# A token mixer behind a windowed attention: tap products added in pairs on VectorE, transposed sums stored as they are, and the softmax, the split of u and the stores planned as separate items

## The chip, the cores and the metric

The kernel runs on one core of a Trainium2 chip. The metric is the device time of one execution in microseconds (us), from the first to the last instruction of the program and the little around them. Engines are named as in the profile: PE is TensorE (PEld its weight loads), DVE is VectorE, ACT is ScalarE, POOL is GpSimd, SP is SyncE, which here only issues transfers.

## What is computed

```python
# attention over a window of 7 past rows; B, S, D = 8, 4096, 192; 8 heads of 24 channels
w = softmax(weight_gen, axis=-1)                        # [8, 4096, 8, 7]
out[b, s, h, :] = sum_k w[b, s, h, k] * x_pad[b, s + k, h, :]
# then, with x = out, a token mixer and a channel mixer
h  = relu(x.transpose(0, 2, 1) @ w_tok1) @ w_tok2       # 4096 -> 256 -> 4096
u  = x + h.transpose(0, 2, 1)
out = u + relu(u @ w_ch1) @ w_ch2                       # 192 -> 1536 -> 192
```

The weights of the mixers are 64-bit floats. From the 32-bit numbers made of them the products on PE are built in three parts, high by high, high by low and low by high (token1 of the first two batches is plain).

## The kernel before

The 8 x 4096 rows are cut into 64 chunks of 512 rows (`g` or `m`, 0 to 63), eight to a batch. A chunk is held as [128 partitions, 4 rows, 192 channels]. For each chunk there are these steps:

- **Softmax** (L163 to L180), for two chunks at a time: five VectorE instructions and one exponential on ScalarE.
- **Attention** (`attention`, L196): seven tap products, x shifted by k rows times the weight of tap k (`product`, L203), each 128x768 on VectorE. The first goes into the sum `xa`; each of the other six goes into one of four buffers `pr` (PR, L46), and GpSimd issues a transfer that adds the buffer to `xa` in memory (`add_dma`, L220). The next addition into the same `xa` waits until the one before has landed, and a product that needs a buffer waits until an addition has emptied it.
- **Turning**: VectorE transposes the finished `xa` in blocks of 32x32 (`turn`, L283), ScalarE moves the blocks with 24 copies of 32x128 (`move`, L289, L293) into `ts`, and ScalarE's queue stores `ts` to memory (`keep`, L272). Later SP loads it as `xb` with two transfers (`load_xt`, L309). For the first eight chunks PE does the turning (`turn_first`).
- **token1** (L480 to L502): PE multiplies the first token weights with `xa`; VectorE adds the result up over the eight chunks of a batch in `h1s`. From batch 2 on `xa` is first split into a high and a low part, `xh` (L257 on ScalarE, L260 on VectorE).
- **token2** (`token2`, L506): ten matmuls (L513) into PSUM, three VectorE additions with `xb` (L520 to L522) that make u, and its split into high and low parts (two VectorE and four ScalarE instructions, L524 to L529), all issued at once behind one another.
- **Channel mixer**, three quarters per chunk: `channel1` (24 matmuls, L544 and L549, into two PSUM tiles `ph`; each is then evicted as `h` by ScalarE, L552, and VectorE, L553), and `channel2` (20 matmuls, L567, into the one PSUM tile `acc`) for the quarter before.
- **Store** (`store`, L572): three VectorE additions empty `acc` (L577 to L579), two transposes (L581, L582), 12 ScalarE copies (L589), two transfers on ScalarE's queue (L599).

During the prologue and the first eight chunks ScalarE and VectorE also convert the weights from 64 bits (`convert`, L137; `convert_w2`, L395 on, with L404 and L405 for its high and low part).

PSUM has three tiles of kind `w`, used in turn by `ph`, token1 and token2, and one `acc`. So PE's next `channel1` waits for the VectorE instruction at L553 of an earlier quarter, and the first `channel2` of a chunk waits for L579 of the chunk before.

Each engine works its instructions off in the order in which they were written. That order is made while the program is built, by a planner in the same file: it keeps an estimated clock per engine (`at`), issues the PE work quarter by quarter (the loop at L884), and between them fills VectorE and ScalarE with items of waiting lists (`chains`), each item with an estimated cost (`pump`, L663). `ISSUE`, `ADD`, `LOAD`, `KEEP` (L606 to L610) are its estimates for transfers; an addition in memory is taken to be done 5 us after its issue. The attention of a chunk may run up to RUN = 12 chunks ahead of its token2 (L41, L743).

Of the kernel before, what the change touches and what calls it, by code (L numbers as in the profile page):

```python
# [21 lines left out]
def mixer_kernel(ctx: ExitStack, tc: tile.TileContext, x, wg, wt1, wt2, wc1, wc2, out):  # L22
# [22 lines left out]
    TAPS = [(k,) for k in range(K)]  # L45
    PR = 4  # L46

# [115 lines left out]
    def softmax(m):  # L163
        t = wgt.pop(m)
        nt = SM * CT
        wn = p1.tile([P, K, nt, H], F32, tag="wn", name="wn")
# [4 lines left out]
        yield "v", 540, lambda: nc.vector.tensor_reduce(mx, t, axis=AX.X, op=ALU.max)  # L171
        yield "v", 540, lambda: nc.vector.tensor_sub(t, t, bc(mx))
        yield "a", 470, lambda: nc.scalar.activation(t, t, AF.Exp)
        yield "v", 540, lambda: nc.vector.tensor_reduce(mx, t, axis=AX.X, op=ALU.add)
# [5 lines left out]
        yield "v", 540, lambda: nc.vector.tensor_mul(wn.rearrange("p k t h -> p t h k"), t, bc(mx))  # L180
# [15 lines left out]
    def attention(ms):  # L196

        done, sums = {}, {}
        cost = 70 + CT * D * 1.05
# [8 lines left out]
        def one(m, k, first):  # L208
            t = new_xa(m) if k == 0 else late.tile([P, CT, D], F32, tag="pr", name="pr", bufs=PR)
            product(m, k, t)  # L210
            if first:
                sums[m] = t
            else:
                prt[m] = t
# [11 lines left out]
        for ks in TAPS:  # L226
            for m in ms:
                for k in ks:
# [5 lines left out]
                    if k != ks[0]:  # L234
                        yield "v", cost, lambda m=m: add_dve(m)
                if ks[0] != 0:
                    yield "n", 0, lambda m=m: add_dma(m)

        def summed(m):
            xa_at[m] = done[m]  # L240
            add_chain(two_parts(m), done[m])
            state["summed"] = m
        for m in ms:
            yield "n", 0, lambda m=m: summed(m)
# [6 lines left out]
    def two_parts(m):  # L251
# [9 lines left out]
        if m // NCH >= F1:  # L261
            yield "a", 760, hi
            yield "v", 876, lo
# [6 lines left out]
    Q = 32  # L270

    def keep(m, t):  # L272

        xst[m] = dram.tile([2, P, N], F32, name=f"xs{m}")
        nc.scalar.dma_start(xst[m][0], t[:, 0, :])
        nc.scalar.dma_start(xst[m][1, DC:P], t[DC:P, 1, :])

    def turns():

        for m in range(NCH, NG):  # L280
            box = {}

            def turn():  # L283
                box["t"] = late.tile([P, CT, D], F32, tag="t", name="t")
                nc.vector.transpose(box["t"].rearrange("p c d -> p (c d)"), xat[m].rearrange("p c d -> p (c d)"))  # L285
                box["s"] = late.tile([P, 2, N], F32, tag="ts", name="ts")
                state["turned"] = m

            def move(part):  # L289
                t = box["t"].rearrange("p c (d j) -> p c d j", j=Q)  # L290
                for d, n in part:
                    dst, to = (box["s"][:, 0], d * Q) if d < DA // Q else (box["s"][:, 1], DC + d * Q - DA)
                    nc.scalar.copy(dst[to:to + Q, :].rearrange("p (c n j) -> p c n j", c=CT, j=Q)[:, :, n, :],  # L293
                                   t[n * Q:(n + 1) * Q, :, d, :])
            yield "gate", 0, lambda: state["summed"] >= m
            yield "w", 0, lambda: xa_at[m]
            yield "v", 876, turn
            every = [(d, n) for d in range(D // Q) for n in range(P // Q)]
            for at_ in range(0, len(every), MOVES):
                part = every[at_:at_ + MOVES]  # L300
                yield "u", 300 * len(part), lambda part=part: move(part)

            def last():
                keep(m, box["s"])
                state["kept"] = m
                return max(at["act"], at["pe"]) + KEEP
            yield "w", 0, last

    def load_xt(m):  # L309

        xbt[m] = p1.tile([P, 2, N], F32, tag="xb", name="xb", bufs=2)
# [644 lines left out]
```

## Time and profile before

| what | value |
|---|---|
| median of 3 runs | 2341.88 us (2335.44 to 2349.58) |
| the profiled execution's own time | 2351.83 us |
| its span, first to last instruction | 2350.1 us |
| mean granted TensorE clock | 0.970 |
| busy: PE, DVE, ACT, POOL | 93%, 69%, 60%, 13% of the span |
| transfers issued by GpSimd (additions in memory) | 31.6% of the 16 DMA engines' time |
| transfers issued by SP; by ScalarE | 29.8%; 8.0% |

The profiled execution is one run, and is 9.95 us slower than the median of the runs. PE is busy nearly all the time, so what counts is where PE stands idle, or works at a lower granted clock, and who it then waits for. In a row of the profile the last part says how long the engine stood idle just before such instructions, and after `<-` what ended that.

### The profile page before, as it was taken

How to read it: one execution, taken by the hardware profiler on the slowest of the kernel's cores; microseconds unless marked ns; L12 is line 12 of the kernel's file. 1: busy time of each engine (PE TensorE's matmuls, PEld its weight loads, DVE VectorE, ACT ScalarE, POOL GpSimd, SP SyncE). 2: the span in 40 equal slices, each digit the busy share in tenths (PEclk: the TensorE clock that was granted, in tenths of full speed). 3: DMA queues.
4: the chain of work that ended last, by engine and by line, in shares of the span. 5: the costliest groups of instructions: out<-in, count | busy, mean ns of one | idle time of the engine just before them, and what ended most of it. 6: DMA issues, size and time to landing. Idle time of an engine off the chain costs nothing.

```text
span 2350.1 us, 28487 instructions
## 1 busy us (share of the span) xinstructions
PE 2188.0 (93%) x10464; PEld 1703.4 (72%) x10464; DVE 1624.9 (69%) x1932; ACT 1405.7 (60%) x2969; POOL 304.4 (13%) x359
## 2 busy tenths in 40 slices
PE   8968999899899999999999999999999999999998
PEld 5746777677677777777777777777777777777776
DVE  8886888686666767667777776676776667544443
ACT  5546786566666656665556766555666656544444
POOL 0011222111111111111111111111111111000000
PEclk9978999899999999999999999999999999999999
DMA  7677989896778787677887777778777777212210
GB/s 283 221 197 211 247 223 233 215 250 164 214 200 219 203 187 203 168 207 195 199 223 185 186 189 204 194 192 223 172 184 204 192 195 173 93 63 63 63 57 21
DMA packets 131820, 429.65 MB, mean 183 GB/s; under 512 B 16232, under 2 KB 26728, under 8 KB 116320
## 3 DMA queue, kind: packets, MB, share of 16 engines
q0 software_dynamic: 49536, 140.53, 31.6%
q1 hardware_dynamic: 58016, 237.74, 29.8%
q10 hardware_dynamic: 24128, 49.56, 8.0%
q8 instruction: 82, 1.34, 0.2%
q14 instruction: 58, 0.48, 0.1%
HBM read 225.13 MB, written 70.52 MB: 126 GB/s over the span
## 4 chain that ended last, share of the span: by engine, by line
PE 34%; DMA 29%; DVE 17%; ACT 14%; issue 4%; ACTq 1%; SPq 0%; POOLq 0%; DVEq 0%
DMA xa<-pr 24%; PE acc L567 13%; PE ph L544 8%; ACT ts L293 6%; DVE h L553 5%; PE ph L549 4%; ACT out_tile L589 4%; DVE pr L203 3%; PE tapsum L336 3%; PE up L513 2%; ACT h L552 2%; DMA xt<-in_x_dram 2%; DVE t L285 1%; DVE xa L203 1%; DMA val<-s 1%
## 5 line engine op out<-in xcount | busy, mean ns | idle before, releaser
L567 PE MATMUL acc<-h,w2s 128*128 128x512 f32 x3840 | 936.9, 399 | 34.4 <-DVE ua L579 34.3
L567 PEld LDWEIGHTS acc<-h,w2s 128*128 128x128 f32 x3840 | 713.9, 190 | 247.0 <-issue 88.6
L552 ACT ACTIVATE h<-ph 128x1024 fp32r<-128x1024 f32 x384 | 373.2, 1024 | 332.8 <-PE ph L549 312.5
L553 DVE SCALAR_TENSOR_TENSOR h<-ph,h 128x1024 fp32r<-128x1024 f32 x384 | 450.9, 1215 | 171.9 <-ACT h L552 171.9
L221 POOL DMA_DIRECT2D xa<-pr x336 | 292.7, 874 | 1554.7 <-DVE pr L203 806.7
L293 ACT COPY ts<-t 32x128 f32<-32x128 f32 x1344 | 397.5, 296 | 47.8 <-DMA xs<-ts 10.0
L203 DVE TENSOR_TENSOR pr<-xt,wn 128x768 f32<-128x768 f32 x336 | 310.0, 946 | 157.6 <-DMA xa<-pr 156.6
L544 PE MATMUL ph<-a_hi,w1a_hi 128*128 128x512 f32 x768 | 316.2, 412 | 71.7 <-DVE h L553 64.2
L544 PE MATMUL ph<-a_hi,w1a_lo 128*128 128x512 f32 x768 | 310.8, 405 | 0.0
L544 PE MATMUL ph<-a_lo,w1a_hi 128*128 128x512 f32 x768 | 310.5, 404 | 0.1
L544 PEld LDWEIGHTS ph<-a_hi,w1a_hi 128*128 128x128 f32 x768 | 151.2, 197 | 110.6 <-DVE h L553 71.2
L589 ACT COPY out_tile<-ua 32x256 f32<-32x256 f32 x512 | 206.8, 404 | 8.5 <-DVE ua L582 1.8
L513 PE MATMUL up<-w,h 128*128 128x512 f32 x640 | 161.7, 400 | 21.0 <-ACT w L404 10.6
L544 PEld LDWEIGHTS ph<-a_lo,w1a_hi 128*128 128x128 f32 x768 | 151.1, 197 | 34.1 <-DVE a_lo L527 1.2
L544 PEld LDWEIGHTS ph<-a_hi,w1a_lo 128*128 128x128 f32 x768 | 151.5, 197 | 30.1
L549 PE MATMUL ph<-c_hi,w1c_hi 64*128 64x512 f32 x768 | 172.7, 446 | 0.0
L513 PEld LDWEIGHTS up<-w,h 128*128 128x128 f32 x640 | 123.4, 193 | 48.5 <-ACT w L404 11.0
L549 PE MATMUL ph<-c_lo,w1c_hi 64*128 64x512 f32 x768 | 152.3, 393 | 0.0
L549 PE MATMUL ph<-c_hi,w1c_lo 64*128 64x512 f32 x768 | 151.4, 391 | 0.0
L520 DVE TENSOR_TENSOR uc<-up,xb 64x512 f32<-64x512 f32 x64 | 44.4, 693 | 130.7 <-ACT out_tile L589 103.4
L549 PEld LDWEIGHTS ph<-c_hi,w1c_hi 64*128 64x128 f32 x768 | 72.4, 185 | 78.5 <-issue 69.4
L483 PE MATMUL th<-xh,w 128*128 128x384 f32 x384 | 113.7, 360 | 10.5 <-ACT w L157 9.3
(77 smaller groups left out, 1963.4 us busy)
## 6 DMA issues: line engine op xcount, KB each, us to landing
xa<-pr POOLq DMA_DIRECT2D x336, 384.0 KB, 5.9
w<-s SPq DMA_DIRECT2D x96, 1024.0 KB, 6.3
xt<-in_x_dram SPq DMA_DIRECT2D x56, 960.0 KB, 9.2
out_dram<-out_tile ACTq DMA_DIRECT2D x128, 192.0 KB, 3.1
raw<-in_moe_w_tok_dram SPq DMA_DIRECT2D x16, 1024.0 KB, 6.6
xs<-ts ACTq DMA_DIRECT2D x62, 256.0 KB, 5.2
xb<-xs SPq DMA_DIRECT2D x62, 256.0 KB, 7.1
s<-w POOLq DMA_DIRECT2D x8, 1024.0 KB, 9.8
```

The costliest lines, as they stand in the source:

```text
L203: nc.vector.tensor_mul(t.rearrange("p t (h g) -> p (t h) g", h=H).rearrange("p (o n) g -> p o n g", o=1), x_k, w)
L221: nc.gpsimd.dma_start(xat[m].rearrange("p t d -> p (t d)"), sums[m].rearrange("p t d -> p (t d)"), accum_op=ALU.add)
L293: nc.scalar.copy(dst[to:to + Q, :].rearrange("p (c n j) -> p c n j", c=CT, j=Q)[:, :, n, :], t[n * Q:(n + 1) * Q, :, d, :])
L336: nc.tensor.matmul(ps[:, n, 0:half * D], ident, prs[k][:, n * half:(n + 1) * half, :], start=k == 0, stop=k == K - 1)
L483: nc.tensor.matmul(th[:, r, 0:2 * D], w[:, c, 0, rs], xh[:, c, :], start=c == 0, stop=False)
L513: nc.tensor.matmul(up[:, n, :], h1[:, k, d], w[:, k, l, :], start=k == 0 and j == 0, stop=k == KR - 1 and j == len(steps) - 1)
L544: nc.tensor.matmul(ph[p][:, j, :], w[:, fs], u, start=n == 0, stop=False)
L549: nc.tensor.matmul(ph[p][:, j, :], w[rows, p * P:(p + 1) * P], u[rows], start=False, stop=n == 2)
L552: nc.scalar.activation(h[:, :, 0, :], ph[p], AF.Relu)
L553: nc.vector.scalar_tensor_tensor(h[:, :, 1, :], ph[p], 0.0, h[:, :, 0, :].bitcast(F32), op0=ALU.max, op1=ALU.subtract)
L567: nc.tensor.matmul(acc[:, n, :], w2s[:, f, d], h[:, j, l, :], start=f == 0 and i == 0, stop=f == NF - 1 and i == len(steps) - 1, skip_grou ...
L589: nc.scalar.copy(dst, src[to:to + Q].rearrange("p (c n k d) -> p c n k d", c=CT, n=2, d=Q)[:, :, n])
```

## The change

1. **Pairs of taps.** `TAPS` becomes (0), (1, 2), (3, 4), (5, 6): both products of a pair go to `pr` buffers, VectorE adds them (`add`, L221 of the changed kernel), and one addition in memory takes the sum. That is three additions in memory per chunk instead of six. Chunks 8 to 15 use (0), (1, 2), (3, 4), (5), (6). In all 336 additions in memory become 176, and 160 VectorE additions of 128x768 are new.
2. **Transposed sums as they are.** The 32x32 transpose writes `t` as [128, 6, 128], SP stores it whole, and SP loads `xb` with six transfers, each 32 partitions by four runs of 128 numbers (512 bytes). The 24 ScalarE copies per chunk go. The columns of a chunk thereby come in another order, which `w2` and the final store follow.
3. **Own items.** Softmax is a waiting list of its own (`softmaxes`), one pair of chunks ahead, with two `wn` buffers; the split of u (`u_parts`) and the store become lists too; token2 evicts its high half first. Output stores go to SP's queue instead of ScalarE's.
4. **Planner.** `ADD` is 7000 instead of 5000, `LOAD` 8000 instead of 5000, most item costs are new; `need` can name lists that go first; token2 may be issued without the split of u done, and the planner asks for the split before the next `channel1`.

```diff
-    TAPS = [(k,) for k in range(K)]
     PR = 4
+    FIRST = 6
+    EARLY = 2
+    TAPS = [(0,), (1, 2), (3, 4), (5, 6)]
+    TAPS0 = [(0,), (1, 2), (3, 4), (5,), (6,)]
...
-        wn = p1.tile([P, K, nt, H], F32, tag="wn", name="wn")
+        wn = p1.tile([P, K, nt, H], F32, tag="wn", name="wn", bufs=2)
...
-        def add_dve(m):
+        def add(m):
             nc.vector.tensor_add(sums[m], sums[m], prt.pop(m))
-            pr_free.append(at["dve"])
+            pr_free.append(at["dve"] + cost)
...
-        for ks in TAPS:
+        for ks in (TAPS if ms[0] >= EARLY * NCH else TAPS0):
             for m in ms:
...
                     yield "v", cost, lambda m=m, k=k: one(m, k, k == ks[0])
-                    if k != ks[0]:
-                        yield "v", cost, lambda m=m: add_dve(m)
-                if ks[0] != 0:
+                if len(ks) > 1:
+                    yield "v", cost, lambda m=m: add(m)
+                if ks[0] > 0:
                     yield "n", 0, lambda m=m: add_dma(m)
...
-                box["t"] = late.tile([P, CT, D], F32, tag="t", name="t")
-                nc.vector.transpose(box["t"].rearrange("p c d -> p (c d)"), xat[m].rearrange("p c d -> p (c d)"))
-                box["s"] = late.tile([P, 2, N], F32, tag="ts", name="ts")
+                t = box["t"] = late.tile([P, D // Q, CT * Q], F32, tag="t", name="t")
+                nc.vector.transpose(t.rearrange("p d (c b) -> p d c b", c=CT),
+                                    xat[m].rearrange("p c (d a) -> p d c a", a=Q))
...
+            def keep():
+                xst[m] = dram.tile([P, D // Q, CT * Q], F32, name=f"xs{m}")
+                nc.sync.dma_start(xst[m], box["t"])
+                state["kept"] = m
...
-        nc.sync.dma_start(xbt[m][:, 0, :], s[0])
-        nc.sync.dma_start(xbt[m][DC:P, 1, :], s[1, DC:P])
+        for d in range(D // Q):
+            dst = t[d * Q:(d + 1) * Q, 0] if d < DA // Q else t[DC + d * Q - DA:DC + (d + 1) * Q - DA, 1]
+            nc.sync.dma_start(dst.rearrange("a (n j) -> a n j", n=P // Q),
+                              s[:, d, :].rearrange("(n a) j -> a n j", a=Q))
...
-            nc.scalar.dma_start(rows.rearrange("(k p c) d -> p k (c d)", k=OB, c=CT),
+                nc.sync.dma_start(rows.rearrange("(k p c) d -> p k (c d)", k=OB, c=CT),
...
-    ISSUE, ADD = 1000, 5000
+    ISSUE, ADD = 900, 7000
...
+        need(lambda: g + 1 in ut or g + 1 >= NG, ("u", g + 1))
```

What the change moves is seen in the order of instructions on an engine. VectorE before, from the last quarter of chunk 38 to the first of chunk 39 (`h` is the eviction of a quarter, `pr` a product, `h1s` token1's sum, `uc` and `ua` the store's additions):

```order
L553 SCALAR_TENSOR_TENSOR h<-ph,h 128x2x512 x2
L203 TENSOR_TENSOR pr<-xt,wn 128x768 x4
L494 TENSOR_TENSOR h1s<-th,h1s 128x384
L553 SCALAR_TENSOR_TENSOR h<-ph,h 128x2x512 x2
L203 TENSOR_TENSOR pr<-xt,wn 128x768
L260 TENSOR_TENSOR xh<-xa,xh 128x4x192
L577 TENSOR_TENSOR uc<-acc,uc 64x512
L578 TENSOR_TENSOR uc<-acc,uc 64x512
L579 TENSOR_TENSOR ua<-acc,ua 128x512
```

And VectorE now, from the last quarter of chunk 40 to the first of chunk 41 (`pr<-pr` is the new addition):

```order
L560 SCALAR_TENSOR_TENSOR h<-ph,h 128x2x512 x2
L529 TENSOR_TENSOR a_lo<-ua,a_hi 128x512
L207 TENSOR_TENSOR pr<-xt,wn 128x768
L530 TENSOR_TENSOR c_lo<-uc,c_hi 64x512
L221 TENSOR_TENSOR pr<-pr 128x768
L207 TENSOR_TENSOR pr<-xt,wn 128x768 x2
L221 TENSOR_TENSOR pr<-pr 128x768
L207 TENSOR_TENSOR pr<-xt,wn 128x768
L560 SCALAR_TENSOR_TENSOR h<-ph,h 128x2x512 x2
```

Four products, each with an addition in memory of its own, stood between two evictions; now there are four products, two additions on VectorE and two in memory, with the split of u between them.

PE at the end of batch 0 before, where the first token2 of batch 1 (`up` with `h_2644`) stands ahead of the last quarter of chunk 7 (`acc` is channel2, `ph` channel1):

```order
L549 MATMUL ph<-c_hi,w1c_lo 128x512 x2
L549 MATMUL ph<-c_lo,w1c_hi 128x512 x2
L567 MATMUL acc<-h,w2s 128x512 x20
L513 MATMUL up<-w_2772,h_2644 128x512 x10
L544 MATMUL ph<-a_hi,w1a_hi 128x512
```

PE at the same place now; these `ph` are already the first quarter of chunk 8, which needs the u of this token2:

```order
L556 MATMUL ph<-c_lo,w1c_hi 128x512 x2
L574 MATMUL acc<-h,w2s 128x512 x20
L499 MATMUL th<-xa,val 128x192 x16
L511 MATMUL up<-w_2458,h_2801 128x512 x10
L551 MATMUL ph<-a_hi,w1a_hi 128x512
```

The last two token1 of batch 1 (`th`, x16) and its first token2 now stand directly before the quarter that uses them; at the end of batch 1 the token2 of chunk 16 stands directly before its own first quarter too. In the other chunks token2 stays a quarter or more ahead.

SP's queue before, over one chunk and a half late in the program:

```order
L85 DMA xt<-in_x_dram 128x1920 x2
L383 DMA w_10798<-s_81 128x2048
L102 DMA wg<-in_weight_gen_dram 128x224 x2
L415 DMA w_10989<-s_82 128x2048
L313 DMA xb<-xs_8841 128x512
L314 DMA xb<-xs_8841 64x512
```

SP's queue now, over a similar stretch (`out_dram` is the output, `xs` the transposed sum that is kept):

```order
L381 DMA w_11955<-s_81 128x2048
L607 DMA out_dram<-out_tile 32x2x768 x2
L413 DMA w_12058<-s_82 128x2048
L308 DMA xb<-xs_9992 32x4x128 x6
L291 DMA xs_12137<-t 128x768
L89 DMA xt<-in_x_dram 128x1920 x2
L291 DMA xs_12198<-t 128x768
```

The loads of the token weights (`w`) and of `xb` now stand behind output stores that wait for ScalarE and behind stores of `t` that wait for VectorE.

More of the change, by code (lines that the diff above doesn't have):

```diff
@@ L681, in pump @@
                     start = max(at["act"], c.wait)
-                    if kind == "s" and scalar or not state["late"] and (start > now + 400 or start + c.item[1] > end):
+                    if kind == "s" and scalar > 1 or not state["late"] and (start > now + 400 or start + c.item[1] > end):
                         continue
@@ L695, in pump, with need @@
             best.issue()
-    def need(what):
+    def need(what, *keys):
         while not what():
@@ L838, in mixer_kernel @@
         pass
+    run(u_parts(0))
+    free["u"] = 0.0
     load_xt(2)
-    stream = attention_stream()
-    run(last, c2_it, islice(stream, 6))
-    chains += [Chain(stream), Chain(turns())]
+    att = attentions()
+    run(last)
+    run(c2_it)
+    run(islice(att, FIRST))
+    chains[0:0] = [Chain(att), Chain(turns()), Chain(soft)]
     add_chain(load_w1(NCH))
@@ L880, in token2_ready @@
     def token2_ready(m):
-        return m < NG and m not in ut and m in w2t and m in xbt and m // NCH in h1t \
+        return state["token2"] < m < NG and m in w2t and m in xbt and m // NCH in h1t \
             and h1_at[m // NCH] <= at["pe"] + 300 and state["stored"] >= m - 2
```

194 lines of the change are left out of this document (103 added, 91 removed).

## The prediction

> **What bounds the kernel now.** First the page's busy times and the windows of four stretches: the prologue, the first chunks with the conversion of weights, the main stretch, and the end without attention. The columns are the window, its length, busy us (and instructions) of PE, PEld, DVE, ACT and POOL, then granted clock, DMA share and GB/s.
>
> ```profile
> PE 2188.0 (93%) x10464; PEld 1703.4 (72%) x10464; DVE 1624.9 (69%) x1932; ACT 1405.7 (60%) x2969; POOL 304.4 (13%) x359
> ...
> 0.00:180.00 180.00, 146.32 (x612) 104.50 (x612) 150.75 (x136) 92.38 (x111) 13.59 (x22) 0.92 0.75 235
> 180.00:600.00 420.00, 381.77 (x1822) 298.70 (x1822) 328.66 (x395) 287.20 (x626) 76.93 (x91) 0.96 0.87 222
> 600.00:2000.00 1400.00, 1322.22 (x6396) 1038.21 (x6394) 985.07 (x1214) 865.92 (x1945) 213.90 (x246) 0.97 0.77 195
> 2000.00:2350.10 350.10, 337.70 (x1638) 261.97 (x1636) 160.47 (x188) 160.19 (x288) 0.00 (x0) 0.99 0.19 59
> ```
>
> PE is the bound, and what can be won is its idle time and its lost clock. In the main stretch it is idle 1400 - 1322.2 = 77.8 us and loses 3% of 1400 = 42 us of clock, 120 us in all. Next the waits of PE and VectorE in that stretch (who waited for whom, us in total, times, longest).
>
> ```profile
> PE ph L544 <- DVE h L553: 43.4, 17, 4.6
> PE acc L567 <- DVE ua L579: 34.3, 18, 3.6
> ...
> DVE pr L203 <- DMA xa<-pr: 143.0, 57, 8.2
> DVE uc L520 <- ACT out_tile L589: 64.2, 19, 4.3
> DVE c_lo L525 <- ACT c_hi L524: 54.8, 20, 3.9
> DVE t L285 <- DMA xa<-pr: 54.7, 17, 4.1
> DVE h L553 <- ACT h L552: 46.9, 48, 3.4
> ```
>
> Two waits, both for VectorE, make up all of PE's 77.8 us; and VectorE's dearest wait is for the additions in memory, 143.0 + 54.7 = 197.7 us. The timeline joins the two, for each of PE's two kinds of wait (start, us, engine, instruction, idle before it).
>
> ```profile
> 1554.14 0.87 POOL L221 DMA_DIRECT2D xa<-pr  x1 [2.90 <-DVE c_lo L525]
> 1563.44 0.87 POOL L221 DMA_DIRECT2D xa<-pr  x1 [8.43 <-DMA xa<-pr]
> ...
> 1562.94 0.96 DVE L203 TENSOR_TENSOR pr<-xt,wn 128x768 f32<-128x768 f32 x1 [7.74 <-DMA xa<-pr]
> 1563.81 2.35 DVE L553 SCALAR_TENSOR_TENSOR h<-ph,h 128x1024 fp32r<-128x1024 f32 x2
> ...
> 1565.09 0.50 PE L544 MATMUL ph<-a_hi,w1a_hi 128*128 128x512 f32 x1 [3.43 <-DVE h L553]
> ...
> 1577.30 0.98 DVE L285 STREAM_TRANSPOSE t<-xa 128x768 f32<-128x768 f32 x1 [3.22 <-DMA xa<-pr]
> ...
> 1580.60 0.69 DVE L579 TENSOR_TENSOR ua<-acc,ua 128x512 f32<-128x512 f32 x1
> ...
> 1581.44 0.47 PE L567 MATMUL acc<-h,w2s 128*128 128x512 f32 x1 [1.08 <-DVE ua L579]
> ```
>
> A product waits 7.74 us for a free `pr` buffer; the evictions stand behind it on VectorE; PE waits 3.43 us for them. Then the transpose waits 3.22 us for the last addition, the emptying of `acc` stands behind it, and PE waits again. GpSimd's two rows are 9.3 us apart: additions into a sum follow each other at that pace. The last view is the stretch of single chunks, from one chunk's first eviction to the next's.
>
> ```profile
> 1432.10:1463.70 31.60, 31.60 (x159) 24.97 (x158) 22.56 (x29) 27.15 (x70) 1.77 (x2) 1.00 0.63 194
> 1463.70:1500.10 36.40, 34.25 (x162) 26.62 (x161) 26.71 (x35) 16.21 (x28) 7.84 (x9) 0.95 0.99 243
> 232.90:265.00 32.10, 32.10 (x160) 25.44 (x159) 30.40 (x36) 26.81 (x53) 6.59 (x8) 1.00 0.99 266
> ```
>
> A chunk in which PE never waits takes 31.6 us. The next one, with nine additions in memory and the DMA engines busy to 0.99, takes 36.4. The third shows VectorE busy 30.40 of 32.10 us with PE still unbroken.
>
> **The change part by part.** The sum is made against the profiled execution, 2351.83 us (span 2350.1 and 1.7 around it), which lies 9.95 above the median of the runs.
>
> *Pairs, main stretch.* The rows for it, in the main stretch and on the page:
>
> ```profile
> L553 DVE SCALAR_TENSOR_TENSOR h<-ph,h 128x1024 fp32r<-128x1024 f32 x243 | 285.3, 1214 | 46.9 <-ACT h L552 46.9
> L203 DVE TENSOR_TENSOR pr<-xt,wn 128x768 f32<-128x768 f32 x240 | 221.1, 946 | 143.9 <-DMA xa<-pr 143.0
> ...
> L221 POOL DMA_DIRECT2D xa<-pr x336 | 292.7, 874 | 1554.7 <-DVE pr L203 806.7
> L293 ACT COPY ts<-t 32x128 f32<-32x128 f32 x1344 | 397.5, 296 | 47.8 <-DMA xs<-ts 10.0
> ...
> xa<-pr POOLq DMA_DIRECT2D x336, 384.0 KB, 5.9
> ```
>
> Six evictions make a chunk, so the stretch holds 243 / 6 = 40.5 chunks of 34.6 us; at 31.6 us they would take 1280, which is the same 120 us again. Before, two chunks side by side need 12 additions, two at a time at 9.3 us: 56 of the pair's 69 us, in bursts. Now they need six: 28 us of about 64. And a product now finds its buffer taken only when the addition seven VectorE instructions (7 x 0.92 = 6.4 us, evictions not counted) earlier has not landed, where it was four products (3.7 us); a landing takes 5.9 us after an issue of 0.87. So most such waits should go, and those in front of the transpose too, since a sum's last addition has only two ahead of it. What it adds: three VectorE instructions of 221.1 / 240 = 0.92 us, 2.8 us per chunk. VectorE then works 985.07 / 40.5 + 2.8 = 27.1 us of a chunk of 31.6, or 86%; the third window above had 95% and PE was not held. What is late next is VectorE's denser queue itself. I take 0.7 us per chunk as left over, between 0 and half of the present 3.0, nearer to the lower end since the row with 95% has none: 40.5 x (3.0 - 0.7) = **-92 us**.
>
> Here a rule of the Trainium skill speaks against the additions.
>
> ```profile
> L203 DVE TENSOR_TENSOR pr<-xt,wn x336: 909/947/962, 147.6 to 1974.5; 128x768 f32<-128x768 f32 x168
> ```
>
> The products read two operands from SBUF, as the new additions do, while GpSimd issues 336 transfers of 0.87 us each; the longest product took 962 ns against a median of 947, so none was held for the length of an issue, and the sum has nothing for it. The Trainium skill, "SBUF — State Buffer", § Who interferes with whom, says that a VectorE instruction with two SBUF inputs blocks against a GpSimd instruction that reads SBUF, one waiting out the whole of the other. If issues counted as such, the 160 additions could lose up to 160 x 0.87 = 139 us on VectorE; this trace does not bear that out for issues.
>
> A second rule bears on the 42 us. The chunk at 1463.70 has 2.15 us of idle PE in all (36.40 - 34.25) and yet a granted clock of 0.95. The Trainium skill, "TensorE: Matmul & The Clock Gate", § Why this matters for your kernels, puts the limit for dropping the clock at idle gaps of about 3 us. By that rule alone few gaps here, 35 with 77.7 us or 2.2 us in the mean, would cost clock and the term would be some 40 us smaller; the trace disagrees, so I go by the trace.
>
> *First chunks, 180 to 600 us.* Idle 38.2 us and 4% of 420 = 17 us of clock. Counted over the whole order, chunks 0 to 7 have 61 products and 18 additions where they had 83 products: VectorE has about as much to do, and fewer additions in memory. I take half back, -25. Against it stand the two places where token2 comes directly before the quarter that uses it. The nearest row is the start of the mixer:
>
> ```profile
> 132.90 0.79 PE L544 MATMUL ph<-a_hi,w1a_hi 128*128 128x512 f32 x1 [4.14 <-ACT a_hi L526]
> ```
>
> That is 4.1 us twice, some 2 us of clock each, and for the first up to one landing, 5.9 us, until the last sum of batch 1 is there: +17, between +8 and +25. Together **-8 us**, between -35 and +15.
>
> *ScalarE's copies.* 397.5 us of ScalarE go. ScalarE is not the bound; where VectorE waits for it (64.2 and 54.8 us above) VectorE's delay is already in the 120 us. Nothing more is counted. The transpose is written in another order; its cost lies between the 0.97 us of L285 and, by the product that writes across (0.98) against one that does not (0.63), half as much again:
>
> ```profile
> L285 DVE STREAM_TRANSPOSE t<-xa 128x768 f32<-128x768 f32 x41 | 39.8, 970 | 54.7 <-DMA xa<-pr 54.7
> L180 DVE TENSOR_TENSOR wn<-wg,mx 128x448 f32<-128x448 f32 x19 | 18.6, 976 | 0.7
> L172 DVE TENSOR_TENSOR wg<-wg,mx 128x448 f32<-128x448 f32 x19 | 11.9, 625 | 0.7
> ```
>
> I take 0.97; at 1.5 us VectorE would have 0.5 us less room per chunk, still under 90%.
>
> *SP's queue.* Per chunk SP issues seven transfers more (four `xb`, one `xs`, two outputs). Behind a waiting output store stand the loads of `w` and `xb`.
>
> ```profile
> xb<-xs SPq DMA_DIRECT2D x62, 256.0 KB, 7.1
> wg<-in_weight_gen_dram SPq DMA_DIRECT2D x64, 112.0 KB, 11.8
> ```
>
> `xb` is wanted about a chunk after its issue; it lands in 7.1 us now, and the rows of 896 bytes of `wg` in 11.8. That leaves 20 us for any wait in the queue: 0. If that cover goes, VectorE and PE wait for `xb` (rival D).
>
> *Prologue and end.* The same conversions, and two products more ahead of the first eviction; at the end VectorE and ScalarE are half idle. 0, give or take 6.
>
> Sum: -92 - 8 = -100. 2351.8 - 100 = 2251.8 for an execution like the profiled one, **2242 us** against the median. Its own range is 2195 to 2290: left-over per chunk 0 to 1.5 us (-29 to +32), first chunks -27 to +23.
>
> **Rivals.** *A, the waits move.* VectorE's queue at 86% holds PE at other places, and half of the main stretch's loss stays, with no gain at the start: -60 + 8, about 2290; up to 2325. For it: chunks 8 to 31 catch up on attention put off from the start, and the order shows up to 11 products and 5 additions in one chunk. Against it: the 95% window.
>
> *B, slower: VectorE becomes the bound.* In the main stretch VectorE is idle 1400 - 985 = 415 us, 197.7 of them for additions in memory; the other 217, 5.4 us per chunk, are waits for PE and ScalarE. If the planner cannot fill these, a chunk takes 27.1 + 5.4 = 32.5 us plus what remains of the waits for memory, now 4.9. The point of change is a remainder of 2.1 us. At 3.0 us the chunk takes 35.5: 40.5 x 0.9 = +36, about 2378. Against it: the first window above has VectorE idle 9 us and PE unbroken, so those waits are mostly spare time.
>
> *C, better.* PE unbroken from 600 on and the starts gained: -120 - 32, about 2190.
>
> *D, the loads come late.* `xb` in pieces of 512 bytes behind waiting stores; if it comes 3 us late in each of 56 chunks with a 2 us loss of clock in half of them, that is +224 and eats the gain twice over; at 1.8 us without any loss of clock it takes 100 and the time stays. Against it: 20 us of room.
>
> **How the numbers follow.** Forecast 0.63, A 0.14, B 0.08, C 0.10, D 0.05. The range reaches down to C and up to most of A: 2185 to 2322. About 0.5% is what a measurement of this kernel can tell from no change, so 2330 to 2354 is the same. Faster: the forecast, A and C, 0.87; slower: B and half of D, 0.10; the same 0.03.
>
> **What would show it.** Right: VectorE's waits for `xa<-pr` in the main stretch fall below 50 us, PE's idle time there below a third of 77.8, the clock to 0.99, chunks at 32 to 32.5 us, and two gaps of 4 to 10 us in front of L551 near the ends of chunks 7 and 15. Wrong: PE waiting for L560 as often as now with VectorE near 95% busy (A, B), or VectorE waiting for `xb` (D).

## The result, and the profile after

The changed kernel takes **2249.53 us** (median of 4 runs, 2247.49 to 2250.37), the kernel before beside it 2345.73 us (2335.44 to 2360.57). The ratio is 0.9584, with a 95% interval of 0.953 to 0.9638. The forecast was 2242 us, in a range of 2185 to 2322. The profiled execution has a span of 2245.7 us, 104.4 less than before; the sum forecast 100. The medians lie 96.2 apart.

The page of the changed kernel: the busy times, the products, the additions on VectorE, the transpose, and the landing time of the additions in memory.

```profile
PE 2161.4 (96%) x10464; PEld 1685.4 (75%) x10464; DVE 1755.6 (78%) x2092; ACT 1011.0 (45%) x1625; POOL 163.0 (7%) x199
...
L207 DVE TENSOR_TENSOR pr<-xt,wn 128x768 f32<-128x768 f32 x336 | 311.4, 946 | 7.4 <-DMA xa<-pr 7.1
...
L221 DVE TENSOR_TENSOR pr<-pr 128x768 f32<-128x768 f32 x160 | 152.4, 953 | 3.4
...
L285 DVE STREAM_TRANSPOSE t<-xa 128x768 f32<-128x768 f32 x56 | 54.2, 969 | 72.5 <-DMA xs<-t 70.0
...
xa<-pr POOLq DMA_DIRECT2D x176, 384.0 KB, 4.6
```

The row of the products on the page of the kernel before:

```profile
L203 DVE TENSOR_TENSOR pr<-xt,wn 128x768 f32<-128x768 f32 x336 | 310.0, 946 | 157.6 <-DMA xa<-pr 156.6
```

VectorE waited 156.6 us for additions in front of products before, and 7.1 now. The median addition lands 4.6 us after the start of its issue instead of 5.9 (the page counts from the start, so the issue of 0.86 us is part of it). But a new wait of 70.0 us stands in front of the transpose: `t` has one buffer, and is stored from directly now, so the next transpose waits until that store has landed.

Where the 104 us are is seen when both traces are cut at the same chunks. Six evictions `h` on VectorE make a chunk, so the first eviction of chunk 12 and that of chunk 54 are marks that both have. The windows of before (to chunk 12, to chunk 54, to the end):

```profile
0.00:598.40 598.40, 526.49 (x2426) 401.89 (x2427) 477.81 (x530) 379.19 (x737) 90.52 (x113) 0.95 0.83 226
598.40:2046.80 1448.40, 1369.42 (x6635) 1075.28 (x6634) 1008.71 (x1244) 894.75 (x2007) 213.90 (x246) 0.98 0.75 193
2046.80:2350.10 303.30, 292.11 (x1406) 226.21 (x1404) 138.43 (x160) 131.75 (x227) 0.00 (x0) 0.99 0.17 52
```

And of the changed kernel at the same marks:

```profile
0.00:559.40 559.40, 515.22 (x2392) 394.26 (x2393) 480.33 (x527) 276.84 (x396) 49.33 (x66) 0.96 0.69 199
559.40:1942.40 1383.00, 1354.01 (x6670) 1064.83 (x6669) 1136.85 (x1405) 602.19 (x1005) 113.63 (x133) 0.99 0.64 173
1942.40:2245.70 303.30, 292.18 (x1406) 226.31 (x1404) 138.39 (x160) 131.94 (x228) 0.00 (x0) 0.99 0.19 52
```

The end is the same to the digit. The 42 chunks of the middle gained 65.4 us, of which 50 are idle time of PE (79.0 to 29.0); the prologue and the first twelve chunks gained 39.0. The forecast had 92 and 8. The work at the first mark is not quite the same: six token1 with split sums stood before it, and four do now. One takes PE 2.25 us, so for the same work the middle gained some 70 us and the part before it some 35. What is not idle time is clock.

What VectorE and PE still wait for in the main stretch (600 to 2000 us) of the changed kernel:

```profile
DVE h L560 <- ACT h L559: 95.5, 44, 7.3
DVE t L285 <- DMA xs<-t: 51.9, 11, 6.6
...
DVE pr L207 <- DMA xa<-pr: 4.7, 2, 2.4
...
PE ph L551 <- DVE h L560: 6.6, 4, 3.2
PE th L481 <- DMA w<-s: 6.3, 3, 2.6
PE th L482 <- DVE w L162: 5.6, 2, 2.8
PE th L481 <- ACT w L161: 2.7, 1, 2.7
PE ph L551 <- ACT a_hi L527: 2.6, 1, 2.6
```

VectorE's 143.0 us in front of products are 4.7. PE's two waits for VectorE, 77.7 us together, are 6.6. More than half of what PE still waits for is new on the list: the token weights, `w`, loaded and split too late (6.3 + 5.6 + 2.7 us). All that PE still waits for before chunk 54 comes before chunk 32, as the window from that chunk's first eviction to chunk 54's shows:

```profile
1243.50:1942.40 698.90, 698.82 (x3475) 551.70 (x3474) 563.31 (x694) 309.77 (x520) 53.02 (x62) 1.00 0.62 166
```

The timeline of a chunk in this undisturbed part, with the order that the section on the change showed:

```profile
1265.73 2.35 DVE L560 SCALAR_TENSOR_TENSOR h<-ph,h 128x1024 fp32r<-128x1024 f32 x2
...
1268.60 0.95 DVE L207 TENSOR_TENSOR pr<-xt,wn 128x768 f32<-128x768 f32 x1
...
1270.07 0.94 DVE L221 TENSOR_TENSOR pr<-pr 128x768 f32<-128x768 f32 x1
...
1270.94 1.81 DVE L207 TENSOR_TENSOR pr<-xt,wn 128x768 f32<-128x768 f32 x2
1271.54 0.87 POOL L225 DMA_DIRECT2D xa<-pr  x1 [32.43 <-DVE pr L221]
1272.78 0.96 DVE L221 TENSOR_TENSOR pr<-pr 128x768 f32<-128x768 f32 x1
...
1274.75 2.36 DVE L560 SCALAR_TENSOR_TENSOR h<-ph,h 128x1024 fp32r<-128x1024 f32 x2
```

VectorE's products and additions follow each other without a bracket, that is without a wait, and the next pair of evictions starts on time.

The new wait, in the timeline around its longest case:

```profile
577.26 0.97 DVE L285 STREAM_TRANSPOSE t<-xa 128x768 f32<-128x768 f32 x1
...
579.56 6.59 SPq L308 DMA_DIRECT2D xb<-xs  x6
...
588.30 0.34 SPq L291 DMA_DIRECT2D xs<-t  x1
...
593.75 0.98 DVE L285 STREAM_TRANSPOSE t<-xa 128x768 f32<-128x768 f32 x1 [8.48 <-DMA xs<-t]
...
597.14 2.35 DVE L560 SCALAR_TENSOR_TENSOR h<-ph,h 128x1024 fp32r<-128x1024 f32 x2
598.41 0.50 PE L551 MATMUL ph<-a_hi,w1a_hi 128*128 128x512 f32 x1 [2.86 <-DVE h L560]
```

The sum is turned by 578.2. SP then issues six pieces of `xb` for 6.59 us, and `t`'s store only at 588.30. The next transpose waits 8.48 us until it has landed, the evictions stand behind it on VectorE, and PE waits 2.86 us. It is the old mechanism with another transfer. SP's queue also shows in the largest gap of the first chunks:

```profile
395.28 5.96 SPq L291 DMA_DIRECT2D xs<-t  x2
...
399.91 0.98 DVE L285 STREAM_TRANSPOSE t<-xa 128x768 f32<-128x768 f32 x1 [3.79 <-DMA xs<-t]
...
401.29 0.94 SPq L370 DMA_DIRECT2D val<-s  x2
...
405.98 1.30 PE L499 MATMUL th<-xa,val 128*128 128x192 f32 x3 [7.08 <-DMA val<-s]
...
416.63 0.50 PE L551 MATMUL ph<-a_hi,w1a_hi 128*128 128x512 f32 x1 [1.43 <-ACT a_hi L527]
```

The second store of `t` stands in SP's queue until its transpose is done at 400.9; behind it stand the token1 weights `val`, and PE waits 7.08 us for them.

### The profile page after: what moved, and what is told of

Read it like the earlier page. It is cut to its first block, busy times and chain, and to the rows that moved or that the text cites. A ratio compares the mean times of both kernels' runs of the same rounds, so it can differ in the third digit from the quotient of the medians.

```text
span 2245.7 us, 27289 instructions
## 1 busy us (share of the span) xinstructions
PE 2161.4 (96%) x10464; PEld 1685.4 (75%) x10464; DVE 1755.6 (78%) x2092; ACT 1011.0 (45%) x1625; POOL 163.0 (7%) x199
## 4 chain that ended last, share of the span: by engine, by line
PE 77%; DVE 10%; DMA 6%; issue 3%; ACT 3%; SPq 0%; POOL 0%; ACTq 0%; DVEq 0%; POOLq 0%
PE acc L574 32%; PE ph L551 19%; PE ph L556 11%; PE up L511 5%; PE tapsum L331 3%; PE th L481 3%; DVE h L560 2%; DMA xa<-pr 2%; PE th L499 2%; DMA xs<-t 2%; DVE pr L207 1%; PE th L482 1%; ACT out_tile L596 1%; DMA xt<-in_x_dram 1%; ACT h L559 1%
## 5 line engine op out<-in xcount | busy, mean ns | idle before, releaser
L574 PE MATMUL acc<-h,w2s 128*128 128x512 f32 x3840 | 926.5, 396 | 1.3 <-ACT h L559 1.0
L574 PEld LDWEIGHTS acc<-h,w2s 128*128 128x128 f32 x3840 | 706.3, 188 | 210.1 <-issue 67.8
L560 DVE SCALAR_TENSOR_TENSOR h<-ph,h 128x1024 fp32r<-128x1024 f32 x384 | 451.3, 1216 | 201.1 <-ACT h L559 199.4
L551 PE MATMUL ph<-a_hi,w1a_hi 128*128 128x512 f32 x768 | 307.0, 400 | 25.1 <-DVE h L560 15.3
L551 PE MATMUL ph<-a_lo,w1a_hi 128*128 128x512 f32 x768 | 304.5, 397 | 1.3 <-DVE a_lo L529 1.3
L551 PE MATMUL ph<-a_hi,w1a_lo 128*128 128x512 f32 x768 | 303.8, 396 | 0.0
L225 POOL DMA_DIRECT2D xa<-pr x176 | 151.2, 859 | 1515.6 <-DVE pr L221 1185.8
L551 PEld LDWEIGHTS ph<-a_hi,w1a_hi 128*128 128x128 f32 x768 | 146.7, 191 | 58.0 <-DVE h L560 18.0
L551 PEld LDWEIGHTS ph<-a_lo,w1a_hi 128*128 128x128 f32 x768 | 146.7, 191 | 35.7 <-DVE a_lo L529 4.9
L551 PEld LDWEIGHTS ph<-a_hi,w1a_lo 128*128 128x128 f32 x768 | 147.1, 192 | 28.5
L221 DVE TENSOR_TENSOR pr<-pr 128x768 f32<-128x768 f32 x160 | 152.4, 953 | 3.4
L285 DVE STREAM_TRANSPOSE t<-xa 128x768 f32<-128x768 f32 x56 | 54.2, 969 | 72.5 <-DMA xs<-t 70.0
```

What stands on the lines that cost most here:

```text
L225: nc.gpsimd.dma_start(xat[m].rearrange("p t d -> p (t d)"), sums[m].rearrange("p t d -> p (t d)"), accum_op=ALU.add)
L551: nc.tensor.matmul(ph[p][:, j, :], w[:, fs], u, start=n == 0, stop=False)
L560: nc.vector.scalar_tensor_tensor(h[:, :, 1, :], ph[p], 0.0, h[:, :, 0, :].bitcast(F32), op0=ALU.max, op1=ALU.subtract)
L574: nc.tensor.matmul(acc[:, n, :], w2s[:, f, d], h[:, j, l, :], start=f == 0 and i == 0, stop=f == NF - 1 and i == len(steps) - 1, skip_grou ...
```

## The experiments

The theories, as the expectations name them: **M**, the additions in memory are too many, and halving them takes the stall away; **P**, the stall is the planner's too low estimate of an addition, so that products are put into VectorE's queue before their buffers are free; **S**, the copies taken from ScalarE bring the gain. Later came **E**: VectorE waited because the planner took an addition for done too early, and fewer additions or a right estimate each cure that; and **T**: what the changed kernel loses against the pairs alone is VectorE's wait for the single `t`, where rival **O** blames the order of the work instead.

The table cuts all traces at the marks used above and at chunk 32; the last two columns are VectorE's waits for additions in memory and for `t`'s store over the whole span. All in us.

| kernel | median | ratio to before (95%) | to chunk 12 | 12 to 32 | 32 to 54 | rest | additions | `t` |
|---|---|---|---|---|---|---|---|---|
| before | 2345.73 | 1 | 598.4 | 697.2 | 751.2 | 303.2 | 217.4 | 0 |
| changed | 2249.53 | 0.9584 (0.953 to 0.9638) | 559.4 | 684.1 | 698.9 | 303.3 | 9.6 | 70.0 |
| before, pairs alone | 2230.76 | 0.9508 (0.9485 to 0.9531) | 566.5 | 660.9 | 698.9 | 303.3 | 45.2 | 0 |
| before, estimate alone | 2232.22 | 0.9518 (0.9488 to 0.9549) | 558.7 | 665.3 | 698.4 | 303.6 | 26.0 | 0 |
| before, both | 2246.99 | 0.9592 (0.9554 to 0.9631) | 572.3 | 674.2 | 699.4 | 303.7 | 43.9 | 0 |
| before, estimate 9000 | 2306.47 | 0.982 (0.9769 to 0.9871) | 565.7 | 701.6 | 713.9 | 321.3 | 7.5 | 0 |
| changed, single taps | 2254.92 | 0.9606 (0.9578 to 0.9634) | 575.8 | 664.7 | 698.4 | 307.8 | 97.3 | 31.1 |
| changed, copies back | 2222.49 | 0.9474 (0.9449 to 0.9499) | 559.0 | 661.7 | 694.8 | 303.2 | 1.7 | 0 |
| changed, two `t` | 2229.80 | 0.952 (0.9487 to 0.9553) | 550.5 | 671.8 | 702.1 | 303.2 | 10.1 | 0 |
| changed, paced turning | 2236.91 | 0.9556 (0.9511 to 0.9602) | 555.6 | 680.8 | 697.0 | 303.2 | 8.0 | 7.9 |
| changed, estimate 5000 | 2273.52 | 0.9709 (0.9677 to 0.9741) | 597.7 | 674.0 | 699.1 | 303.2 | 15.9 | 124.0 |
| two `t`, estimate 5000 | 2219.25 | 0.9439 (0.9395 to 0.9483) | 559.7 | 654.9 | 699.6 | 303.2 | 22.2 | 0 |
| two `t`, single taps | 2241.76 | 0.9544 (0.95 to 0.9588) | 571.2 | 661.6 | 698.4 | 308.0 | 102.6 | 0 |
| two `t`, short first list | 2234.77 | 0.9516 (0.9473 to 0.9559) | 554.2 | 686.5 | 695.5 | 303.2 | 12.2 | 0 |

The kernels have not all done the same number of token1 at a mark. Six stand before chunk 12 in the kernel before, three or four in the others. With single taps in the changed kernel, and with 9000, two or three fewer stand before chunk 54 than elsewhere; with single taps that is the 4.5 us by which the rest is longer.

### Pairs alone

```diff
-    TAPS = [(k,) for k in range(K)]
+    TAPS = [(0,), (1, 2), (3, 4), (5, 6)]
```

> The kernel before with the pairs of taps alone: 168 additions in memory instead of 336, and 168 additions on VectorE; all else, ScalarE's copies and the planner's old numbers too, as before. Theory M (the additions in memory carried the gain, through VectorE's waits for them): most of the 96 us, so 2255 to 2285 us, VectorE's waits for xa<-pr below 80 us where they were 217 in all. Theory P (the planner's new numbers and lists carried it): no gain, 2330 to 2355. Theory S (ScalarE's copies carried it): no gain either.

Measured: 2230.76 us, better than M asked for, and 19 us below the whole change by the medians (the two intervals just touch). Its page:

```profile
L203 DVE TENSOR_TENSOR pr<-xt,wn 128x768 f32<-128x768 f32 x336 | 314.0, 948 | 35.3 <-DMA xa<-pr 34.4
...
xa<-pr POOLq DMA_DIRECT2D x168, 384.0 KB, 4.5
```

The median addition lands 4.5 us after the start of its issue, where the planner takes 1.0 + 5.0 = 6.0. From chunk 32 the loss is gone, and from 600 to 2000 us PE no longer waits for L553 or L579 at all. This one edit is enough for the gain; the rest of the change adds nothing to it, and S has no room.

### The estimate alone

```diff
-    ISSUE, ADD = 1000, 5000
+    ISSUE, ADD = 900, 7000
```

> The kernel before with only the planner's estimate of an addition in memory raised from 5 to 7 us (and its issue from 1.0 to 0.9). Theory M: the additions are as many and as slow, so the waits only move, 2325 to 2355 us. Theory P: a good part of the gain, 2260 to 2300.

Measured: 2232.22 us. The page has all 336 additions, landing as slowly as before, and the waits of the products fall from 156.6 us:

```profile
L221 POOL DMA_DIRECT2D xa<-pr x336 | 292.8, 873 | 1413.8 <-DVE pr L203 505.8
L203 DVE TENSOR_TENSOR pr<-xt,wn 128x768 f32<-128x768 f32 x336 | 311.4, 947 | 26.7 <-DMA xa<-pr 25.8
...
xa<-pr POOLq DMA_DIRECT2D x336, 384.0 KB, 5.8
```

PE's wait for the evictions from 600 to 2000 us, 43.4 us before:

```profile
PE ph L544 <- DVE h L553: 3.2, 3, 1.2
```

M falls as a statement about the number: a number in the planner does what halving the additions does, to 2 us. P expected a good part of the gain, 2260 to 2300 us, and got all of it. The planner counted 6.0 us from one addition into a sum to the next, which is about the median landing of 5.9 us. But the landings spread, from 3.9 to 13.7 us in the kernel before, with a quarter above 9.0; and from 600 to 2000 us nearly every addition that waited for the one before it was issued about 0.5 us after that had landed, 7.1 us in the mean after its issue. So a sum of six additions was done later than planned. Now the planner counts 7.9. VectorE does the same work, in an order in which the evictions seldom stand behind a product whose buffer is still being read.

### Single taps in the changed kernel

```diff
-    TAPS = [(0,), (1, 2), (3, 4), (5, 6)]
-    TAPS0 = [(0,), (1, 2), (3, 4), (5,), (6,)]
+    TAPS = [(k,) for k in range(K)]
+    TAPS0 = [(k,) for k in range(K)]
```

> The changed kernel with single taps again: 336 additions in memory, none on VectorE; copies gone, new planner. Theory M: most of the gain is lost, 2305 to 2340 us, and VectorE's waits for xa<-pr come back to over 120 us. Theories P and S: at most 15 us lost, below 2265.

Measured: 2254.92 us, M's number missed by 50. The additions are back at 336 and land after 6.5 us, yet the time is that of the changed kernel (0.9606 against 0.9584, inside each other's intervals). VectorE's waits in this kernel:

```profile
DVE h L560 <- ACT h L559: 302.2, 106, 12.2
DVE pr L207 <- DMA xa<-pr: 97.3, 53, 5.7
```

M also asked for over 120 us of these waits; there are 97.3, and they cost PE next to nothing: 48.8 us of them lie in chunks 32 to 54, which take 698.4 us, no more than in the kernels with few of them (694.8 to 702.1). Where such a wait stands decides, not its sum.

### Pairs and the estimate

Both edits above together, in the kernel before.

> The kernel before with the pairs of taps and the planner's 7 us together. Theory E (VectorE waited because the planner took an addition in memory for done too early; fewer additions or a right estimate each cure that, and the two do not add): 2222 to 2238 us, like either alone, and chunks 32 to 53 again at 31.7 us. A rival by which the two gains add (half of the wait each): below 2200, which would need chunks under 31.6 us.

Measured: 2246.99 us, 9 above E's range, with chunks 32 to 54 at 31.8 us each as E says. The two do not add; together they are 15 us slower than either, and the loss stands between the start and chunk 32. The median landing is 5.4 us here, and the planner now counts 7.9.

### ScalarE's copies put back

```diff
             yield "t", 0, keep
+            def again():
+                s = late.tile([P, 2 * P], F32, tag="ts", name="ts")
+                for n in range(MOVES):
+                    nc.scalar.copy(s[0:Q, n * P:(n + 1) * P], ident[0:Q, :])
+            for _ in range(12):
+                yield "u", 600, again
```

The changed kernel with 24 copies per chunk that nothing reads, as many as the change removed.

> The changed kernel with 24 copies of 32x128 per chunk on ScalarE added back as dead work (they read the identity matrix and write a scratch tile; the output is the reference's). Theory S: most of the gain is lost, 2300 to 2340 us. Theories M and P: ScalarE has room, at most 15 us lost, 2245 to 2265.

Measured: 2222.49 us, faster than without them by 27 us, the intervals apart. S falls; the row of the copies on ScalarE:

```profile
L301 ACT COPY ts<-ident 32x128 f32<-32x128 f32 x1344 | 333.8, 295 | 18.7
```

333.8 us of work there cost nothing that can be seen; the time is not above that of two `t` without copies (2229.80 us, below). The copies stand in the list of turnings, behind each store of `t`, so the next transpose is planned later, and VectorE's wait for `t`'s store, 70.0 us in the changed kernel, is gone. This run gave theory T, which the next one tests without the copies.

### Two buffers for `t`

```diff
-                t = box["t"] = late.tile([P, D // Q, CT * Q], F32, tag="t", name="t")
+                t = box["t"] = late.tile([P, D // Q, CT * Q], F32, tag="t", name="t", bufs=2)
```

(`wg` has one buffer instead of two, to make room.)

> The changed kernel with two buffers for the transposed sum t (and one instead of two for the softmax input, to make room). Theory T (what the rest of the change costs against the pairs alone is VectorE's wait, 70 us in all, for the single t that its store still holds): that wait goes, 2220 to 2235 us. Rival O (it is the order of token1 and of the conversions, whatever t does): 2242 to 2255.

Measured: 2229.80 us, as T says; the wait is gone. Of 18.2 us of span, 8.9 are up to chunk 12 and 12.3 from there to 32, with 3.2 given back behind. The intervals of the ratios overlap slightly, and `wg` with one buffer was not run alone.

### Turning paced by the planner

```diff
             yield "t", 0, keep
+            yield "w", 0, lambda: max(at["act"], at["pe"]) + 6000
```

> The changed kernel, where the planner lets the next transpose wait 6 us after the store of t; one buffer, no work added. This is what the dead copies did in passing. Theory T: 2215 to 2235 us, VectorE's wait for xs<-t below 10 us. A rival by which the dead copies helped through ScalarE's or PE's order: as the changed kernel, 2242 to 2255.

Measured: 2236.91 us, between T's upper end and the changed kernel; inconclusive by its interval. The wait is 7.9 us, but chunks 24 to 32 took 14 us more than in the changed kernel: pacing by time puts the transposes somewhere else.

### The estimate back to 5000 in the changed kernel

```diff
-    ISSUE, ADD = 900, 7000
+    ISSUE, ADD = 900, 5000
```

> The changed kernel with the planner's estimate of an addition in memory back at 5 us. With 176 additions each lands 4.6 us after its issue, so 5 us is now right and theory E expects no return of the waits: xa<-pr below 40 us, 2230 to 2260 us. Theory P alone (the number 7 is what counts): 2290 or more.

Measured: 2273.52 us, slower than the changed kernel, so E's range is missed; P alone asked for 2290 or more, which is not reached either. Its page says where:

```profile
L285 DVE STREAM_TRANSPOSE t<-xa 128x768 f32<-128x768 f32 x56 | 54.2, 969 | 136.4 <-DMA xs<-t 124.0 <-DMA xa<-pr 12.4
```

The additions are still no hindrance (15.9 us in all); but the one `t` is waited for 124.0 us. That sums planned to be done earlier come to the transpose closer together is the likely reason; it was not followed up.

### Two `t` and the estimate at 5000

The two edits together.

> The changed kernel with the tile t double-buffered and the planner's estimate of an addition in memory set back from 7000 to 5000 ns; the run with the estimate alone gave 2273.5 us, with VectorE waiting 124.0 us for t's store and 15.9 us for additions. Theory T (that loss is VectorE waiting for the single t): the wait for t's store goes, and the time falls by most of the 43.7 us that separate that run from the one with t doubled alone, to 2225-2250 us. Rival O (the loss is the order of the first 16 chunks that the lower estimate gives, the wait only its mark): the time stays at 2260-2280 us and another wait stands where t's stood.

Measured: 2219.25 us, the lowest of the study, and below T's range. With `t` doubled the lower estimate goes from a loss of 24 us to a gain of 10 (0.9439 to 0.9483 at most, against 0.9487 at least for two `t` with 7000). The transpose's row, to be held against the one above:

```profile
L285 DVE STREAM_TRANSPOSE t<-xa 128x768 f32<-128x768 f32 x56 | 54.0, 964 | 17.3 <-DMA xa<-pr 17.3
```

So the single `t` cost 54 us in that order, and rival O falls. It is 30 us below the changed kernel (the intervals, up to 0.9483 and from 0.953, are apart) and 126 us below before.

### An estimate that is too high

The kernel before, with 900 and 9000.

> The kernel before with the estimate at 900 and 9000 ns (7000 gave 2232.2 us). The additions land after 5.8 us as issued. Theory M2 (the estimate needs only to be no lower than what the additions take; what is above it delays products that nothing waits for at once): 2225-2245 us, VectorE's wait for additions under 25 us. Rival (the estimate has to fit: too high a one delays the transposes and the quarters that need them): over 2250 us, with PE waiting for the products.

Measured: 2306.47 us: M2 falls, and the rival holds by its time, though PE waits for token sums that come late and not for products. VectorE waits 7.5 us for additions, the least of all kernels with the code of before, and the time is 74 us above the one with 7000. The timeline at one end of a batch:

```profile
1251.36 0.56 DVE L492 TENSOR_TENSOR h1s<-th,h1s 128x384 f32<-128x384 f32 x1 [2.55 <-PE th L484]
...
1253.98 4.05 PE L513 MATMUL up<-w,h 128*128 128x512 f32 x10 [2.66 <-DVE h L471]
1258.07 0.69 DVE L520 TENSOR_TENSOR uc<-up,xb 64x512 f32<-64x512 f32 x1 [4.34 <-PE up L513]
...
1260.77 0.79 PE L544 MATMUL ph<-a_hi,w1a_hi 128*128 128x512 f32 x1 [2.75 <-ACT a_hi L526]
```

Token1 of a batch's last chunk, token2 of the next batch and the quarter that uses it come directly behind one another here, with PE idle 2.66 and 2.75 us. That the sums are finished too late for more room is how this is read. The same pair of gaps comes back in the batches after it, at 1514, 1777 and 2040 us.

### Two `t`, single taps

The edits of those two kernels together.

> The changed kernel with t double-buffered and all taps single, so seven products and six additions in memory per half chunk as before the change. If what the additions cost is only the planner's ignorance of them and the single t, this is as fast as t doubled with pairs (2229.8 us): 2222-2245 us. If the halved number of additions is worth something by itself: over 2250 us, with VectorE waiting for additions again.

Measured: 2241.76 us, in the first range, though VectorE waits 102.6 us for additions again. Against two `t` with pairs (2229.80) it is 12 us more by the medians, with intervals that overlap widely. So pairs as such are worth between nothing and some 12 us once planner and buffers are right.

### Two `t`, the short first list

`EARLY` is 1 instead of 2, so chunks 8 to 15 use the pairs.

> The changed kernel with t double-buffered and the first stretch that uses five single taps and pairs shortened from two tokens' chunks to one. If the first 16 chunks lose time on the longer list of taps there: 2215-2228 us. If they lose it on weights and token items that come late, whatever the taps: 2228-2245 us.

Measured: 2234.77 us, in the second range; no gain. The longer list of the first chunks costs nothing that can be seen here.

## Why the prediction was right, step by step

**What bounds the kernel.** Right. The chain from additions that land late over VectorE's queue to PE was the loss: each of two different edits aimed at these waits alone brings 2344 us to 2231 or 2232, and PE's waits for L553 and L579 (77.7 us) to 0 and 3.2. The chunk length that the prediction read from one undisturbed chunk, 31.6 us, is what is reached: 698.9 / 22 = 31.8 us per chunk from chunk 32 on, in the changed kernel, and 694.8 to 702.1 us for these 22 chunks in all other runs but the kernel before (751.2) and the one with 9000 (713.9).

**Pairs.** The mechanism, a product that finds its buffer free, came about (143.0 to 4.7 us). The reason given for it was only half of it. The prediction costed six additions against three and never set the landings beside the estimate in the planner, which had been described ahead of it. The estimate alone takes these waits away too, and single taps in the changed kernel reach the same time with them. Two readings were off. The landing of 5.9 us already contains the issue of 0.87. And GpSimd's two rows 9.3 us apart belong to two different sums: the addition at 1563.44 follows the one at 1550.38 in its sum, 13.1 us later. In the mean of the main stretch the pace into one sum is 7.1 us, so twelve additions, two at a time, take some 43 of the pair's 69 us and not 56.

**The size of the main stretch.** The term was -92 for 40.5 chunks; 42 chunks gave -65, or some -70 for the same work. Left-over was taken as 0.7 us per chunk evenly; in truth it is about nothing from chunk 32 on, where the gain is 52 us, and all of it lies in the twenty chunks before, which gained only 13 (697.2 to 684.1). There PE is idle 29.0 us (26.1 of them after 600 us, and of these 14.6 for the token weights, whose loads the prediction named under SP's queue at 0), and VectorE waits for `t`.

**The first chunks.** -8 forecast, -39 measured up to chunk 12. "Half back" was too careful: PE's idle time up to chunk 12 went from 598.40 - 526.49 = 71.9 to 559.40 - 515.22 = 44.2 us; 4.5 us are the two token1 that moved past the mark, and the remaining 7 are clock. And token2 directly before its quarter cost 1.43 and 2.56 us of waiting in front of L551 (two gaps of 4 to 10 us were forecast), where the split of its high half now comes first. The two sizes erred in opposite directions, by 27 and 31 us, so that the sum was right to 4 us is luck. (The -25 and +17 of this term stand for 27.6 and 18.1 by its own rows, and the ends of its parts added up give 2186 to 2297 and not 2195 to 2290; neither bears on the outcome.)

**SP's queue at 0.** This step failed. The prediction checked what stood behind the output stores, and not who waits for the new store of `t`: it holds the only `t` until it has landed, and holds the loads behind it until its transpose is done. VectorE waited 70.0 us for that store, and PE 7.08 us for `val` behind it, where the term was 0. Taking VectorE's wait away brought 20 us at 7000, with intervals that overlap slightly, and 54 at 5000, where they are apart. It is a smaller case of the same kind as the loss that the change removed.

**ScalarE's copies at 0, the end at 0.** Right, the first by the copies put back, the second by the two rows of 303.30 us.

**The rivals.** B needed VectorE to become the bound. In the middle it was busy 1136.85 of 1383.00 us (82%), and PE lost only 6.6 us to waits for evictions and 5.6 to the split of the token weights. A's mark, PE waiting for L560 as often as before, did not appear; D's, VectorE waiting for `xb`, not either. Of the marks set: waits under 50 us (4.7), clock 0.99 (0.99), PE's idle time under 25.9 (26.1, just missed), chunks of 32 to 32.5 us (1383.00 / 42 = 32.9 over the whole middle, missed).

**What stays open.** Up to chunk 32 the kernels with equal cures differ by up to some 30 us, since each edit of estimate or list gives another order. Why both edits in the kernel before are slower than either is put down to an estimate that is 2.5 us too long, by analogy with 9000 and with 5000 against 7000 under two `t`; that was not tested by itself. The own lists for softmax, split and stores, and the output stores on SP, were not run without the rest of the change.

## What to carry to other kernels

When an order is planned with estimated times, hold each estimate against the landings in the trace, their spread and not only their median, and try other values before making the transfers fewer. Here 6.0 us, the median, put products in front of evictions that PE needed; 7.9 won 4.8% of the time, and 9.9 gave some two thirds of that back. A change that drops a staging copy makes a transfer the last reader of the buffer: ask at once who writes that buffer next, and what queue the transfer stands in. Where a wait stands in its engine's queue decides what it costs, not the sum of the waits.

## What the runs showed of the hardware

**Fewer additions landed sooner.** The same 384 KB land in the median 5.9 us after the start of the issue before, 5.8 with the estimate alone and 6.5 with single taps in the changed kernel; with about half as many additions after 4.6 us in the changed kernel, 4.5 with pairs alone and 5.4 with pairs and the estimate. The order of the work changes them too, and why was not tried.

**Products on VectorE beside GpSimd's issues.** The 336 products of the changed kernel that go to `pr` took from 909 to 960 ns. In the trace 158 of them overlap an issue, with a median of 949 ns, and the others have 948; none was held for an issue of 0.86 us. (Of the 160 new additions only one overlaps an issue at all, so their own times say nothing of this.) The Trainium skill, "SBUF — State Buffer", § Who interferes with whom, has a VectorE instruction with two SBUF inputs and a GpSimd instruction that reads SBUF exclude each other; issuing these transfers is no such instruction by the trace.

**Clock lost to short gaps, and not lost to longer ones.** Two gaps of PE and the 3.8 us behind each, in windows (the clock is the third number from the right). First before:

```profile
1508.10:1510.10 2.00, 0.16 (x1) 0.19 (x2) 1.90 (x4) 1.93 (x7) 0.00 (x0) 1.00 0.00 0
1510.10:1513.90 3.80, 3.80 (x11) 2.98 (x11) 2.85 (x4) 3.70 (x8) 0.00 (x0) 0.60 0.00 0
```

And the changed kernel:

```profile
745.20:747.80 2.60, 0.04 (x1) 0.07 (x1) 2.54 (x4) 0.00 (x0) 0.00 (x0) 1.00 0.42 89
747.80:751.60 3.80, 3.80 (x23) 3.56 (x24) 3.67 (x6) 0.00 (x0) 0.86 (x1) 1.00 0.60 107
```

After 1.9 us of idle time the clock was 0.60 of full speed in the mean of the next 3.8 us; after 2.6 us it stayed at 1.00. The Trainium skill, "TensorE: Matmul & The Clock Gate", § Why this matters for your kernels, puts the limit at about 3 us of idle time. These rows show losses below it, and that the length of the gap alone does not decide; what else does was not tried.
